# Stage A of a chunked Fourier transform in plain float32, in the four 64x64 quarters of the tensor array, in place of a three-product split-float32r form

## The chip, the cores and the metric

One core of a Trainium2 chip runs one program: a tensor engine (PE, with its weight loads listed as PEld), a vector engine (DVE), a scalar engine (ACT), GpSimd (POOL) and a sync engine (SP) that mostly issues transfers. The metric is the device time of one execution in microseconds, lower is better; three runs were made of the kernel before. Every instruction, transfer and semaphore wait of one execution is in the trace, and a one-page profile sums it up. An operation in float32 is written F32 below; F32R is float32r, a float32 format that the tensor engine takes in one pass with fewer mantissa bits, so the kernel splits an F32 number into a high and a low F32R part where it needs full precision.

## The reference

Three layers follow one another. The change touches only the first, and there only its forward transform.

```python
x: (8, 3072, 256)                              # batch, sequence, channels
X = np.fft.rfft(x, axis=1)
y = np.fft.irfft(X * (filt_r + 1j * filt_i), n=3072, axis=1)
# then a token-mixing layer on y
k = relu(xk @ w_k);  v = (k * k) @ w_v;  z = sigmoid(xr @ w_r) * v      # 256 -> 1024 -> 256
# then on all 24576 rows of z
out = max(z @ w1, z @ w2, z @ w3) @ w_out                               # 256 -> 768 -> 256
```

## The kernel before

The transform of length 3072 is cut as 48 x 64, as two stages of matmuls with a stored intermediate. The 64 is itself a pair (j, m) of 2 x 32: sequence index = 64 n + 32 j + m. **Stage A** transforms over n (48 points, real input, 48 real outputs: real and imaginary parts of 24 frequencies g) for each j and m. **Stage B** then works per g on 128 rows, multiplies by the filter, and **stage C** is the inverse of stage B. Stage A writes its output to the DRAM tensor `s1`, stage B reads it from there, stage C writes `s2`, and the later layers read `s2`.

Batch 0 has a transform of its own at the head of the program (`fft_first`, plain F32, nothing else to overlap with). The seven other batches use `fft(b)`: it returns a list of small pieces, and `drive` puts these between the units of the batch before it (the two later layers), each piece having a weight in about microseconds, so that the pieces are spread over that batch in proportion to their weights. The tile framework's scheduler then orders the instructions of each engine. So stage A of batches 1 to 7 runs in between matmuls of the later layers, and the tensor engine always has other work queued.

In `fft(b)` stage A before has 16 steps (`NA = NM // 2`), each for two values of m. Step s loads a tile `xa` of 96 rows (n and j) x 2 x 256 columns (`a_load`, on SP's queue), ACT casts it to the high part `xah`, POOL subtracts to get the low part `xal` (`split`, L178 and L179). One step later `a_mm` runs three F32R matmuls (`mm3`: high weights x high data, high weights x low data, low weights x high data) of 96 rows by 96 outputs by 512 columns into one PSUM bank `pa`, ACT copies the bank to `ao` (L350) and issues the store to `s1` (L351). The 96x96 weight matrix `wa` holds the same 48x48 transform twice, once on the rows of each j, with zeros elsewhere. All matmuls go through the helper `mm` at L153, so the profile names them by their tiles: `pa<-xah,wa_s` and `pa<-xal,wa_s` are stage A, `pa<-x,wa_f` is the plain F32 stage A of batch 0, `pb`, `pe` and `pa<-x,ws` belong to the last layer, `pk`, `pv`, `pr`, `po` to the two later layers, `pb<-xbh,wbc` to stage B.

PSUM has one pool, `ps`, of 8 banks for everything; a bank comes free when ACT or DVE has read it.

Of the kernel before, what the change touches and what calls it, by code (L numbers as in the profile page):

```python
# [9 lines left out]
F32 = mybir.dt.float32  # L10
F32R = mybir.dt.float32r
# [6 lines left out]
N1 = 48  # L18
N2 = 64
NP = 2 * N1  # L20
NG = N1 // 2
NM = N2 // 2
NQ = 4 * NG
NK = 2 * N2


def fft_constants():


    n1 = np.arange(N1)  # L30
    n2 = np.arange(N2)
    wa = np.zeros((NP, 2, 2, NG))
    wi = np.zeros((2, 2, NG, NP))
    for j in range(2):
        for g in range(NG):
            ph = 2 * np.pi * ((n1 * g) % N1) / N1
            if g == 0:
                wa[j::2, 0, j, 0] = 1.0
                wa[j::2, 1, j, 0] = (-1.0) ** n1
                wi[0, j, 0, j::2] = 1.0 / N  # L40
                wi[1, j, 0, j::2] = (-1.0) ** n1 / N
            else:
                wa[j::2, 0, j, g] = np.cos(ph)
                wa[j::2, 1, j, g] = -np.sin(ph)
                wi[0, j, g, j::2] = 2 * np.cos(ph) / N
                wi[1, j, g, j::2] = -2 * np.sin(ph) / N
    wb = np.zeros((2, N2, NG, 2, N2))
    wc = np.zeros((2, N2, NG, 2, N2))
    freq = np.zeros((2, N2, NG), np.int64)
    for g in range(NG):  # L50
        for s in range(N2):
            if g:
                f = g + N1 * s
                th = 2 * np.pi * ((n2 * f) % N) / N
                c, sn = np.cos(th), np.sin(th)
                sg = 1.0 if s < NM else -1.0
                wb[0, :, g, 0, s] = c
                wb[1, :, g, 0, s] = sn
                wb[0, :, g, 1, s] = -sg * sn
                wb[1, :, g, 1, s] = sg * c  # L60
                wc[0, s, g, 0, :] = c
                wc[1, s, g, 0, :] = -sg * sn
                wc[0, s, g, 1, :] = sn
                wc[1, s, g, 1, :] = sg * c
                freq[:, s, g] = f if s < NM else N - f
            else:
                src = 0 if s < NM else 1
                f = N1 * s if s < NM else NG + N1 * (s - NM)
                th = 2 * np.pi * ((n2 * f) % N) / N
                c, sn = np.cos(th), np.sin(th)  # L70
                freq[:, s, g] = f
                if s == 0:
                    wb[0, :, 0, 0, 0] = 1.0
                    wb[0, :, 0, 1, 0] = (-1.0) ** n2
                    wc[0, 0, 0, 0, :] = 1.0
                    wc[1, 0, 0, 0, :] = (-1.0) ** n2
                    freq[1, 0, 0] = N // 2
                else:
                    wb[src, :, 0, 0, s] = c
                    wb[src, :, 0, 1, s] = -sn  # L80
                    wc[0, s, 0, src, :] = 2 * c
                    wc[1, s, 0, src, :] = -2 * sn

    wb = wb.reshape(4, NM, NG, NK).transpose(1, 0, 2, 3)
    wc = wc.reshape(NK, NG, 4, NM).transpose(0, 1, 3, 2)
    return (
        wa.reshape(NP, NQ),
        wi.reshape(NQ, NP),
        wb.reshape(NK, NG, NK),
        wc.reshape(NK, NG, NK),  # L90
        freq.reshape(NK, NG),
    )
# [33 lines left out]
def tile_spectral_moe(ctx: ExitStack, tc, x, filt, ones, wa, wa1, wi, wbc, wb1, wc1, filt1, filt0, mu, w_k, w_v, w_r, w1, w2, w3, w_out, out):  # L126
    nc = tc.nc
    B = x.shape[0]
    P = 128
    C = 256  # L130
# [12 lines left out]
    cpool = ctx.enter_context(tc.tile_pool(name="cpool", bufs=1))  # L143
# [5 lines left out]

    ps = ctx.enter_context(tc.tile_pool(name="ps", bufs=8, space=bass.MemoryType.PSUM))  # L150

    def mm(o, wgt, rhs, start, stop, more=False):
        nc.tensor.matmul(o, lhsT=wgt, rhs=rhs, start=start, stop=stop, skip_group_check=more)  # L153

    def mm3(o, parts, rhs_parts, onto=False, more=False):

# [6 lines left out]
            mm(o, wl, xh, False, k == n - 1, more)  # L163


    wa_s = cpool.tile([NP, 2, NQ], F32R, name="wa_s")
    nc.gpsimd.dma_start(wa_s, wa)
    wi_s = cpool.tile([NQ, 2, NP], F32, name="wi_s")
    mu_s = cpool.tile([P, 2, 2], F32, name="mu_s")
    nmu_s = cpool.tile([P, 2, 2], F32, name="nmu_s")  # L170
# [6 lines left out]
    def split(hi, lo, src, lo_eng=None):  # L177
        nc.scalar.copy(hi, src)  # L178
        (lo_eng or nc.gpsimd).tensor_tensor(lo, src, hi.bitcast(F32), ALU.subtract)  # L179
# [148 lines left out]
    def fft(b):  # L328

        s1 = dp.tile([NM, 4, NG, C], F32, tag="s1", name=f"s1_{b}")  # L330
        s2 = dp.tile([NM, 4, NG, C], F32, tag="s2", name=f"s2_{b}")
        s2_of[b] = s2
        xv = x[b].rearrange("(p m) c -> p m c", m=NM)
        st = {}
        pieces = []

        def a_load(s):
            t = fp.tile([NP, 2, C], F32, tag="fin", name="xa")
            nc.sync.dma_start(t, xv[:, 2 * s : 2 * s + 2, :])
            hi = fp.tile([NP, 2, C], F32R, tag="fhi", name="xah")  # L340
            lo = fp.tile([NP, 2, C], F32R, tag="flo", name="xal")
            split(hi, lo, t, nc.gpsimd)
            st["a", s] = hi, lo

        def a_mm(s):
            hi, lo = st.pop(("a", s))
            p = ps.tile([NQ, 2, C], F32, tag="pm", name="pa")
            mm3(p, [(wa_s[:, 0], wa_s[:, 1])], [(hi, lo)])
            o = fp.tile([NQ, 2, C], F32, tag="fo", name="ao")
            nc.scalar.copy(o, p)  # L350
            nc.scalar.dma_start(s1[2 * s : 2 * s + 2].rearrange("m r g c -> (r g) m c"), o)  # L351

        NA = NM // 2
        NBS = NG // 2
        for s in range(NA + 1):
            def pa(s=s):
                if s < NA:
                    a_load(s)
                if s >= 1:
                    a_mm(s - 1)  # L360
            pieces.append((0.65, pa))

        def b_load(s):
            w = fp.tile([NK, 4, 2, NK], F32R, tag="wbc", name="wbc")
            if b == 1:

                nc.gpsimd.dma_start(w, wbc[:, s])
                wbc_d[s] = dp.tile([NK, 4, 2, NK], F32, tag=f"wbcd{s}", name=f"wbcd{s}", bufs=1)
                nc.scalar.dma_start(wbc_d[s], w.bitcast(F32))
            else:  # L370
                nc.sync.dma_start(w.bitcast(F32), wbc_d[s])
            f = fp.tile([NK, 2, 2, C], F32, tag="filt", name="filt")
            nc.sync.dma_start(f, filt[:, s])
            t = fp.tile([NK, 2, C], F32, tag="fin", name="xb")
            nc.sync.dma_start(t, s1.rearrange("m r g c -> (m r) g c")[:, 2 * s : 2 * s + 2, :])
            hi = fp.tile([NK, 2, C], F32R, tag="fhi", name="xbh")
            lo = fp.tile([NK, 2, C], F32R, tag="flo", name="xbl")
            split(hi, lo, t)
            st["b", s] = w, f, hi, lo

        def b_mm(s):
            w, f, hi, lo = st.pop(("b", s))
            p = ps.tile([NK, 2, C], F32, tag="pm", name="pb")
            for g in range(2):
                mm3(p[:, g], [(w[:, 0, g], w[:, 1, g])], [(hi[:, g], lo[:, g])], g > 0, True)

            fr, fi = f[:, 0], f[:, 1]
            H = NK // 2
            nc.vector.scalar_tensor_tensor(fi[:H], p[H:], -1.0, fi[:H], ALU.mult, ALU.mult)
            nc.vector.tensor_tensor(fi[H:], p[:H], fi[H:], ALU.mult)  # L390
            nc.vector.tensor_tensor(fr, p, fr, ALU.mult)
            (nc.gpsimd).tensor_tensor(fr, fr, fi, ALU.add)
            yh = fp.tile([NK, 2, C], F32R, tag="fhi", name="yh")
            yl = fp.tile([NK, 2, C], F32R, tag="flo", name="yl")
            split(yh, yl, fr)
            st["c", s] = w, yh, yl

        def c_mm(s):
            w, yh, yl = st.pop(("c", s))
            p = ps.tile([NK, 2, C], F32, tag="pm", name="pc")  # L400
            for g in range(2):
                mm3(p[:, g], [(w[:, 2, g], w[:, 3, g])], [(yh[:, g], yl[:, g])], g > 0, True)
            o = fp.tile([NK, 2, C], F32, tag="fo", name="co")
            nc.scalar.copy(o, p)
            nc.scalar.dma_start(s2.rearrange("m r g c -> (m r) g c")[:, 2 * s : 2 * s + 2, :], o)

        for s in range(NBS + 2):
            def pb(s=s):
                if s < NBS:
                    b_load(s)  # L410
                if 1 <= s <= NBS:
                    b_mm(s - 1)
            def pc(s=s):
                if s >= 2:
                    c_mm(s - 2)
            pieces.append((0.65, pb))
            if s == 0:

                pieces.append((6.0, lambda: None))
            pieces.append((0.65, pc))  # L420
        return pieces
# [520 lines left out]
def layout(x, filt_r, filt_i, mu_k, mu_r, w_k, w_v, w_r, w1, w2, w3, w_out):  # L942
    wa, wi, wb, wc, freq = fft_constants()
    C = x.shape[2]
    wah = np.stack(two_parts(wa), axis=1)
    wis = np.zeros((NQ, 2, NP), np.float32)
    wis[:, 0] = wi
    wis[:, 1, 1:] = wi[:, :-1]
# [19 lines left out]
```

## Time and profile before

| | |
|---|---|
| median of three runs | 3239.52 us (3239.22 to 3243.35) |
| span of the profiled execution | 3228.3 us |
| PE busy | 3117.6 us (97%), 19256 matmul records |
| ACT, POOL, DVE busy | 1918.9, 1865.8, 1774.2 us (59%, 58%, 55%) |
| stage A of batches 1 to 7 | 336 F32R matmuls, 112 casts, 112 subtractions, 112 copies |

The page gives the span of the profiled execution from its first to its last instruction. The time of a run holds what lies around the span as well: 3239.52 - 3228.3 = 11.2 us between the median and the span. Busy time of the tensor engine counts the modelled end of each matmul, which lies behind the start of the next one, so how often matmuls start is read from the timeline and not from the mean duration.

### The profile page before, as it was taken

The page shows a single profiled execution, that of the slowest core. Times are in us where ns is not written, and L with a number is a line of the kernel's source. Part 1 is how long each engine was busy: PE and PEld are TensorE (multiplying, and loading weights), DVE is VectorE, ACT ScalarE, POOL GpSimd, SP SyncE. Part 2 cuts the span into 40 slices and gives each one's busy share as a digit, 9 for nine tenths or more (in the row PEclk, how much of TensorE's full clock was granted, in tenths as well). Part 3 has the DMA queues.
Part 4 walks back from the last instruction along what each step waited for, and adds up shares of the span by engine and source line. Part 5 has one row for each costly group of instructions (what it writes and reads, how often), then busy time and mean ns, then how long its engine had stood idle before and what let it go on. Part 6 is the DMA issues. An engine that isn't in the chain of part 4 may idle for free.

```text
span 3228.3 us, 55882 instructions
## 1 busy us (share of the span) xinstructions
PE 3117.6 (97%) x19256; PEld 3039.7 (94%) x19256; DVE 1774.2 (55%) x2882; ACT 1918.9 (59%) x4024; POOL 1865.8 (58%) x1619
## 2 busy tenths in 40 slices
PE   6799899999999999999999999999999999999998
PEld 4799889999999999999999999999999999999998
DVE  4865554556554565456545465445654456555554
ACT  5556556656566566656566556665656666555554
POOL 3545665557555675546756566565655567544443
PEclk8899999999999999999999999999999999999999
DMA  8767786657765676657766577655876657655553
GB/s 283 239 231 220 227 299 202 194 174 259 238 196 187 208 244 201 214 170 234 252 196 186 179 252 246 198 187 166 271 237 189 190 191 242 197 162 163 169 163 123
DMA packets 397783, 676.38 MB, mean 210 GB/s; under 512 B 41920, under 2 KB 153664, under 8 KB 396864
## 3 DMA queue, kind: packets, MB, share of 16 engines
q1 hardware_dynamic: 328336, 585.61, 57.1%
q10 hardware_dynamic: 66752, 78.75, 7.1%
q0 software_dynamic: 2416, 8.46, 0.9%
q8 instruction: 156, 2.56, 0.3%
q14 instruction: 123, 1.01, 0.1%
HBM read 580.51 MB, written 92.14 MB: 208 GB/s over the span
## 4 chain that ended last, share of the span: by engine, by line
PE 79%; DMA 8%; DVE 7%; issue 2%; ACT 2%; POOL 2%; SPq 0%; ACTq 0%; POOLq 0%; DVEq 0%
PE pb L153 18%; PE pk L153 13%; PE pv L153 13%; PE po L153 12%; PE pe L153 8%; PE pa L153 6%; PE pr L153 4%; PE py L153 3%; DMA wbc<-wbcd 3%; DMA ws<-wud 2%; PE pc L153 2%; DVE x L179 1%; DVE sc L665 1%; DMA wbc<-in_wbc 1%; POOL klo L179 1%
## 5 line engine op out<-in xcount | busy, mean ns | idle before, releaser
L153 PE MATMUL pb<-x,ws 128*128 128x384 f32 x3456 | 759.9, 339 | 15.6 <-DMA ws<-wud 12.4
L179 POOL TENSOR_TENSOR hh<-m,hh 128x384 fp32r<-128x384 f32 x384 | 398.7, 1046 | 557.4 <-ACT hh L178 446.1
L179 POOL TENSOR_TENSOR klo<-kr,khi 128x384 fp32r<-128x384 f32 x492 | 518.2, 1060 | 261.0 <-ACT khi L178 246.6
L153 PEld LDWEIGHTS pb<-x,ws 128*128 128x128 f32 x3456 | 600.7, 189 | 31.8 <-ACT u L701 7.1
L633 DVE SCALAR_TENSOR_TENSOR kr<-pk,kr 128x384 f32<-128x384 f32 x512 | 282.1, 554 | 496.3 <-ACT kr L632 495.0
L153 PE MATMUL po<-wo_hi,hh 128*128 128x256 f32 x2304 | 484.9, 283 | 5.9 <-ACT hh L178 3.3
L153 PE MATMUL pv<-khi,ws 128*128 128x384 f32 x2048 | 475.8, 338 | 7.3 <-ACT khi L178 7.2
L153 PEld LDWEIGHTS po<-wo_hi,hh 128*128 128x128 f32 x2304 | 391.3, 190 | 11.1 <-ACT hh L178 6.9
L153 PE MATMUL pe<-x,ws 128*128 128x384 f32 x1728 | 388.6, 337 | 0.0
L178 ACT CAST khi<-kr 128x384 fp32r<-128x384 f32 x512 | 260.6, 512 | 193.3 <-DVE kr L633 164.9
L153 PEld LDWEIGHTS pv<-khi,ws 128*128 128x128 f32 x2048 | 359.8, 188 | 12.7 <-ACT khi L178 11.9
L153 PE MATMUL pk<-xh,wk_hi 128*128 128x384 f32 x1024 | 341.4, 337 | 3.9 <-ACT xh L178 3.9
L153 PE MATMUL pk<-xl,wk_hi 128*128 128x384 f32 x1024 | 344.1, 336 | 0.2 <-DVE xl L179 0.2
L153 PE MATMUL pk<-xh,wk_lo 128*128 128x384 f32 x1024 | 344.0, 336 | 0.0
L632 ACT ACTIVATE kr<-pk 128x384 f32<-128x384 f32 x512 | 249.2, 489 | 117.1 <-PE pk L153 55.8
L153 PE MATMUL po<-wo_lo,hh 128*128 128x256 f32 x1152 | 317.5, 282 | 0.0
L748 DVE TENSOR_TENSOR m<-sc,m 128x384 f32<-128x384 f32 x384 | 311.5, 814 | 10.0
L153 PEld LDWEIGHTS pe<-x,ws 128*128 128x128 f32 x1728 | 298.8, 189 | 0.9 <-DVE sc L747 0.2
L153 PE MATMUL pv<-klo,ws 128*128 128x384 f32 x1024 | 293.0, 338 | 3.9 <-POOL klo L179 3.0
L179 POOL TENSOR_TENSOR xl<-xm,xh 128x768 fp32r<-128x768 f32 x126 | 233.6, 1869 | 101.3 <-ACT xh L178 101.3
L178 ACT CAST hh<-m 128x384 fp32r<-128x384 f32 x384 | 193.8, 515 | 147.9 <-DVE m L748 80.4
L701 ACT COPY v<-pb 128x384 f32<-128x384 f32 x288 | 138.5, 481 | 162.0 <-PE pb L153 156.5
(129 smaller groups left out, 6060.0 us busy)
## 6 DMA issues: line engine op xcount, KB each, us to landing
ws<-wud SPq DMA_DIRECT2D x864, 256.0 KB, 3.4
ws<-wvd SPq DMA_DIRECT2D x512, 256.0 KB, 3.2
filt<-in_filt SPq DMA_DIRECT2D x84, 512.0 KB, 5.1
ws<-wud SPq DMA_DIRECT2D x288, 128.0 KB, 3.5
wbc<-wbcd SPq DMA_DIRECT2D x72, 512.0 KB, 5.1
cin<-s SPq DMA_DIRECT2D x64, 384.0 KB, 4.2
out_dram<-osb ACTq DMA_DIRECT2D x192, 128.0 KB, 3.0
xb<-s SPq DMA_DIRECT2D x85, 256.0 KB, 3.5
```

The costliest lines, as they stand in the source:

```text
L153: nc.tensor.matmul(o, lhsT=wgt, rhs=rhs, start=start, stop=stop, skip_group_check=more)
L178: nc.scalar.copy(hi, src)
L179: (lo_eng or nc.gpsimd).tensor_tensor(lo, src, hi.bitcast(F32), ALU.subtract)
L632: nc.scalar.activation(r, p, AF.Relu)
L633: nc.vector.scalar_tensor_tensor(r, p, 0.0, r, ALU.max, ALU.mult)
L665: eng.tensor_tensor(t, a, b, ALU.subtract)
L701: nc.scalar.copy(st[to], st[of])
L748: nc.vector.tensor_tensor(m, c, m, ALU.max)
```

## The change

Stage A of batches 1 to 7 takes x as it is. A step now covers four values of m: the tile `xa` is 128 rows by 4 x 256, of which rows 0 to 47 hold j = 0 and rows 64 to 111 hold j = 1, loaded by two transfers. The weights are one 48x48 matrix, padded to 48x64, at rows 0 to 47 and again at rows 64 to 111. Four F32 matmuls, each of 48 rows by 64 outputs by 512 columns, are placed by `tile_position` in the four 64x64 quarters of the array: rows by j, columns by c (which half of the four m). The two j write to two PSUM banks. Two copies of 128 x 512 and four stores follow. The casts and the subtractions are gone, as are the buffers of `xah` and `xal`; `xa` takes turns in the buffer named `filt`. The weights of `s1`'s rows in stage B (`wb`) and the matrix of batch 0 are permuted to the new order of rows, which moves no instruction.

```diff
     def mm(o, wgt, rhs, start, stop, more=False, at=None):
-        nc.tensor.matmul(o, lhsT=wgt, rhs=rhs, start=start, stop=stop, skip_group_check=more)
+        nc.tensor.matmul(o, lhsT=wgt, rhs=rhs, start=start, stop=stop, skip_group_check=more, tile_position=at)
...
-    wa_s = cpool.tile([NP, 2, NQ], F32R, name="wa_s")
-    nc.gpsimd.dma_start(wa_s, wa)
+    wa_s = cpool.tile([P, P // 2], F32, name="wa_s")
+    nc.scalar.dma_start(wa_s, wa)
...
-        xv = x[b].rearrange("(p m) c -> p m c", m=NM)
+        xv = x[b].rearrange("(n j m) c -> j n m c", j=2, m=NM)
+        R = P // 2
...
         def a_load(s):
-            t = fp.tile([NP, 2, C], F32, tag="fin", name="xa")
-            nc.sync.dma_start(t, xv[:, 2 * s : 2 * s + 2, :])
-            hi = fp.tile([NP, 2, C], F32R, tag="fhi", name="xah")
-            lo = fp.tile([NP, 2, C], F32R, tag="flo", name="xal")
-            split(hi, lo, t, nc.gpsimd)
-            st["a", s] = hi, lo
+            t = fp.tile([P, 4, C], F32, tag="filt", name="xa")
+            for j in range(2):
+                nc.sync.dma_start(t[j * R : j * R + N1], xv[j][:, 4 * s : 4 * s + 4, :])
+            st["x", s] = t
 
         def a_mm(s):
-            hi, lo = st.pop(("a", s))
-            p = ps.tile([NQ, 2, C], F32, tag="pm", name="pa")
-            mm3(p, [(wa_s[:, 0], wa_s[:, 1])], [(hi, lo)])
-            o = fp.tile([NQ, 2, C], F32, tag="fo", name="ao")
-            nc.scalar.copy(o, p)
-            nc.scalar.dma_start(s1[2 * s : 2 * s + 2].rearrange("m r g c -> (r g) m c"), o)
-
-        NA = NM // 2
+            t = st.pop(("x", s))
+            p = [ps.tile([P, 2, C], F32, tag="pm", name="pa") for _ in range(2)]
+            for c in range(2):
+                for j in range(2):
+                    rows = slice(j * R, j * R + N1)
+                    mm(p[j][c * R : c * R + R], wa_s[rows], t[rows, 2 * c : 2 * c + 2], True, True, True, (j * R, c * R))
+            for j in range(2):
+                o = fp.tile([P, 2, C], F32, tag="fo", name="ao")
+                nc.scalar.copy(o, p[j])
+                for c in range(2):
+                    m = 4 * s + 2 * c
+                    nc.scalar.dma_start(s1[m : m + 2, 2 * j : 2 * j + 2].rearrange("m r g c -> (r g) m c"), o[c * R : c * R + N1])
+
+        NA = NM // 4
...
-            pieces.append((0.65, pa))
+            pieces.append((1.0, pa))
```

The scheduler decides where the matmuls of a step come to stand on the tensor engine. The rows below are the start of stage A of batch 1 on that engine. Before, the three matmuls of a step stand together; `pb_`, `pa_` and `pe_` with numbers are PSUM banks of the last layer:

```order
L153 MATMUL pe_2003<-x_1672,ws 128x384 x3
L153 MATMUL pa<-xah,wa_s 96x512
L153 MATMUL pa<-xal,wa_s 96x512
L153 MATMUL pa<-xah,wa_s 96x512
L153 MATMUL pb_2054<-x_1654,ws 128x384 x3
L153 MATMUL pb_1995<-x_1661,ws 128x384 x3
```

Of the change, the same place on the tensor engine, with the first two steps of stage A:

```order
L153 MATMUL pe_2046<-x_1672,ws 128x384 x3
L153 MATMUL pa<-xa,wa_s 64x512 x2
L153 MATMUL pb_2038<-x_1661,ws 128x384 x3
L153 MATMUL pa_2039<-x_1664,ws 128x384 x3
L153 MATMUL pa<-xa,wa_s 64x512 x2
L153 MATMUL pb_1950<-x_1675,ws 128x384 x3
...
L153 MATMUL pe_2113<-x_1672,ws 128x384 x3
L153 MATMUL pa<-xa,wa_s 64x512 x4
L153 MATMUL pe_2046<-x_1678,ws 128x384 x3
```

The four matmuls of the first step are torn into two pairs with six other matmuls between them (each pair holds the two column quarters of one j, that is of one PSUM bank); the four of the second step stand together. Over the whole program 34 of the 56 steps stand as one group of four, 16 as two pairs and 6 as a three and a one: 78 groups, each with whole-array matmuls ahead of it and behind it. Of the 34 groups of four, 21 take both columns of j = 0 first and 13 alternate between the two j.

On ACT, in the same stretch, before:

```order
L350 COPY ao<-pa 96x512
L178 CAST xah<-xa 96x512
L351 DMA s_1_665<-ao 96x2x256
L738 COPY m<-pb_1950 128x384
```

and of the change:

```order
L353 COPY ao<-pa 128x512
L356 DMA s_1_665<-ao 48x2x256 x2
L353 COPY ao<-pa 128x512
L178 CAST hh<-m 128x384
```

The cast is gone from ACT, and there are two store issues for one.

## Rows read from the trace of the kernel before

**Rows 1.** The page: span, busy shares, granted clock by slices of the span

```profile
span 3228.3 us, 55882 instructions
...
PE 3117.6 (97%) x19256; PEld 3039.7 (94%) x19256; DVE 1774.2 (55%) x2882; ACT 1918.9 (59%) x4024; POOL 1865.8 (58%) x1619
...
PEclk8899999999999999999999999999999999999999
```

**Rows 2.** Windows of one batch: stage A, the pause, stages B and C, the rest

```profile
core 0: us, PE busy (x) PEld busy (x) DVE busy (x) ACT busy (x) POOL busy (x), PEclk, DMA share, GB/s
894.00:998.00 104.00, 102.98 (x619) 99.26 (x618) 52.62 (x86) 68.04 (x144) 63.00 (x54) 1.00 0.63 192
998.00:1070.00 72.00, 71.38 (x455) 70.77 (x454) 37.63 (x65) 42.39 (x91) 33.58 (x32) 1.00 0.58 184
1070.00:1247.00 177.00, 172.72 (x1096) 170.49 (x1095) 107.32 (x171) 105.53 (x222) 118.76 (x100) 0.99 0.73 240
1247.00:1281.00 34.00, 34.00 (x217) 34.00 (x216) 13.30 (x26) 20.47 (x44) 20.06 (x19) 1.00 0.57 178
```

**Rows 3.** Timeline of PE around one step of stage A: start, duration in us

```profile
226.84 0.40 PE L153 MATMUL pa<-xah,wa_s 96*96 96x512 f32 x1
227.08 0.39 PE L153 MATMUL pa<-xal,wa_s 96*96 96x512 f32 x1
227.31 0.40 PE L153 MATMUL pa<-xah,wa_s 96*96 96x512 f32 x1
227.54 0.69 PE L153 MATMUL pb<-x,ws 128*128 128x384 f32 x3
```

**Rows 4.** Groups of PE instructions: stage A of batches 1 to 7, then of batch 0

```profile
L153 PE MATMUL pa<-xah,wa_s 96*96 96x512 f32 x224 | 88.8, 396 | 0.5 <-DVE kr L633 0.5
L153 PE MATMUL pa<-xal,wa_s 96*96 96x512 f32 x112 | 43.9, 392 | 0.0
L153 PE MATMUL pa<-x,wa_f 96*96 96x512 f32 x32 | 15.6, 652 | 2.4 <-DMA x<-in_x 2.4
```

**Rows 5.** Timeline of weight loads in stage A of batch 0, and one F32 matmul

```profile
19.23 0.16 PEld L153 LDWEIGHTS pa<-x,wa_f 96*96 96x96 f32 x1 [0.27 <-issue]
...
22.23 0.16 PEld L153 LDWEIGHTS pa<-x,wa_f 96*96 96x96 f32 x1 [0.27 <-issue]
...
20.09 0.59 PE L153 MATMUL pa<-x,wa_f 96*96 96x512 f32 x1
```

**Rows 6.** Timeline of weight loads around the step of Rows 3

```profile
226.50 0.19 PEld L153 LDWEIGHTS pe<-x,ws 128*128 128x128 f32 x1
226.67 0.16 PEld L153 LDWEIGHTS pa<-xah,wa_s 96*96 96x96 f32 x1
226.85 0.17 PEld L153 LDWEIGHTS pa<-xal,wa_s 96*96 96x96 f32 x1
```

**Rows 7.** Waits of PE from 220 us on: total us, times, longest

```profile
PE pb L153 <- DMA wbc<-wbcd: 20.9, 14, 2.8
PE pb L153 <- DMA ws<-wud: 12.4, 14, 2.9
PE pb L153 <- DMA wbc<-in_wbc: 8.4, 6, 2.3
PE pv L153 <- ACT khi L178: 3.6, 10, 0.5
```

**Rows 8.** Groups on ACT and POOL, and transfers, of stage A

```profile
L178 ACT CAST xah<-xa 96x512 fp32r<-96x512 f32 x112 | 69.6, 621 | 5.5 <-DMA xa<-in_x 5.5
L350 ACT COPY ao<-pa 96x512 f32<-96x512 f32 x112 | 65.1, 581 | 52.9 <-PE pa L153 51.4 <-PE pb L153 1.5
L179 POOL TENSOR_TENSOR xal<-xa,xah 96x512 fp32r<-96x512 f32 x112 | 150.4, 1343 | 134.1 <-ACT xah L178 128.8 <-PE ps L153 3.5 <-issue 1.8
L351 ACTq DMA_DIRECT2D s<-ao x112: 311/312/383, 228.4 to 2548.0; - x112
xa<-in_x SPq DMA_DIRECT2D x112, 192.0 KB, 3.6
```

More of the change, by code (lines that the diff above doesn't have):

```diff
@@ L82, in fft_constants @@
                     wc[1, s, 0, src, :] = -2 * sn
-    wb = wb.reshape(4, NM, NG, NK).transpose(1, 0, 2, 3)
+    wb = wb.reshape(2, 2, NM, NG, NK).transpose(2, 1, 0, 3, 4)
     wc = wc.reshape(NK, NG, 4, NM).transpose(0, 1, 3, 2)
     return (
-        wa.reshape(NP, NQ),
+        wa.transpose(0, 2, 1, 3).reshape(NP, NQ),
         wi.reshape(NQ, NP),
@@ L150, in tile_spectral_moe, with mm @@
     ps = ctx.enter_context(tc.tile_pool(name="ps", bufs=8, space=bass.MemoryType.PSUM))
-    def mm(o, wgt, rhs, start, stop, more=False):
-        nc.tensor.matmul(o, lhsT=wgt, rhs=rhs, start=start, stop=stop, skip_group_check=more)
+    def mm(o, wgt, rhs, start, stop, more=False, at=None):
+        nc.tensor.matmul(o, lhsT=wgt, rhs=rhs, start=start, stop=stop, skip_group_check=more, tile_position=at)
     def mm3(o, parts, rhs_parts, onto=False, more=False):
@@ L944, in layout @@
     C = x.shape[2]
-    wah = np.stack(two_parts(wa), axis=1)
+    w48 = wa.reshape(N1, 2, 2, 2 * NG)[:, 0, 0]
+    wat = np.zeros((128, 64))
+    wat[:N1, :N1] = wat[64 : 64 + N1, :N1] = w48
+    wah = wat.astype(np.float32)
     wis = np.zeros((NQ, 2, NP), np.float32)
```

## Prediction

> **What bounds the kernel now.** First the page: the tensor engine is busy for 97% of the span and its clock is granted in full after the first two slices, while ACT, POOL and DVE are each below 60% [rows 1]. Next the windows of one batch, by stage. In the stretch that holds stage A the tensor engine is busy 102.98 of 104 us; in the pause and in the rest it is as full; only where stages B and C run is it idle for 4.3 us of 177 [rows 2]. So in the stage that changes, the tensor engine is the limit, and nothing else can give much: 1.0 us of idle time a batch, 7 us over seven. The list of waits says the same for the whole program: its largest entries are transfers of stage B's weights and of the last layer's, and the largest one on ACT is 3.6 us [rows 7]. A step of stage A is therefore worth the time during which it holds the array, and that is read from the starts in the timeline, not from the mean durations: three F32R matmuls start at 226.84, 227.08 and 227.31 and the next one behind them at 227.54 [rows 3]. That is 0.70 us a step, or 0.233 us for 512 columns.
>
> **What is removed.** 16 steps x 7 batches = 112 steps, 336 matmuls (224 and 112 in the groups [rows 4]): 112 x 0.70 = 78.4 us of the array. 69.6 us of casts leave ACT and 150.4 us of subtractions leave POOL [rows 8]. Neither engine is waited for in stage A by more than the 7 us above, so I value both at 3 us, with 0 and 7 as bounds.
>
> **What is added on the array.** Batch 0 already runs stage A in F32, in the whole array. The code issues 16 matmuls there and the trace has 32 records [rows 4]: an F32 matmul is two passes, each with its own weight load. From the load at 19.23 to that at 22.23 there are eight loads, seven intervals: 3.00 / 7 = 0.4286 us a pass, 0.857 us a matmul of 512 columns [rows 5]. The new stage A has 56 steps of four such matmuls, 224 matmuls and 448 passes. A pass of 48 rows and 64 outputs I cost like the one of 96 by 96, because the number of columns that stream through is the same. All depends on how many passes run side by side, which no row of this trace shows: every matmul in it takes the whole array. The bounds are the four matmuls in the time of one, and one after another.
>
> The two passes of a matmul follow one another in its quarter, and in the timelines matmuls start in the order in which they are written. If that holds between quarters too, the first pass of the second matmul cannot start before the second pass of the first one, and that one waits until its quarter is free. The passes then form a staircase: two passes side by side at a time, and a group of n matmuls takes n + 1 pass times, not 2. For the groups of the new order this is 34 x 5 + 32 x 3 + 6 x 4 + 6 x 2 = 302 pass times, 302 x 0.4286 = 129.4 us: 51.0 us more than the 78.4 us removed. All quarters side by side: 78 groups x 0.857 = 66.9 us, 11.5 us less. One after another: 448 x 0.4286 = 192.0 us, 113.6 us more. I take the staircase, because it needs only what the rows show of order and of passes, and some overlap of quarters.
>
> **What is added around each group.** Before each of the 78 groups and behind it the array changes from whole to quarters and back. Today a load runs under the matmul before it (226.67, 0.17 us ahead of the start of its matmul at 226.84) and a matmul starts 0.16 us before the recorded end of the one ahead of it (0.40 long, next start 0.235 later; in F32 0.59 against 0.43) [rows 3, 5, 6]. If a switch costs nothing, this stays so: 0. If the array must run empty and then load, each group loses 0.16 + 0.16 on entry and 0.16 + 0.19 on exit: 0.67 us, 52 us in all. I take the middle, 0.34 us a group or 26 us, since no row is nearer to one end. [...]
>
> **The rest.** The two copies of a step are as many and as wide as before (112 of 0.58 us [rows 8]; the partitions grow from 96 to 128, the columns don't). ACT issues 224 stores for 112, 112 x 0.312 = 35 us of issue time against 69.6 us of casts: ACT still gains. SP issues 112 loads of 192 KB as before, 3.6 us to land [rows 8], and a step is asked for one piece ahead, now about twice as far apart (104 / 16 = 6.5 us before), so the load stays hidden; were it not, each step would wait for what is left of 3.6 us. `xa` now shares the two buffers of the filter tiles: stage B's first filter load waits for the last matmuls of stage A, but a pause of 72 us lies between [rows 2]. The pieces of stage A weigh 9.0 for 11.05, so stages B and C spread over some 6% more of the batch. Their waits for weights (20.9 + 8.4 us [rows 7]) may move by some us either way; I take 0, bounds -10 and +10. A step now takes two PSUM banks at once, which the torn groups already show.
>
> **Sum.** -78.4 + 129.4 + 26 - 3 = +74 us. The profiled span of 3228.3 becomes 3302, and with the 11.2 us that lie around it the time is 3314 us, 2.3% slower.
>
> **Rivals.**
> 1. All quarters side by side, which ends on the other side. -11.5 us on the array, -3 us elsewhere, plus the switches: 3225 us where these are free, 3277 us where they cost 0.67 us. For it: nothing in the rows says that the second pass of one quarter must hold up another quarter. Against it: starts are in order wherever the trace shows them. It is faster by over 0.2% (6.5 us, about what a measurement of this kernel can tell) only if a switch costs less than (14.5 - 6.5) / 78 = 0.10 us a group. [...]
> 2. The quarters give nothing: 448 passes one after another, +113.6 us and the switches, 3350 to 3402 us. For it: no matmul in the trace ever overlaps another by more than its 0.16 us. Against it: only that the work would fit side by side.
> 3. Only quarters of different rows overlap, columns of the same rows don't. Then a pair of one j takes 4 pass times, the 21 groups that take one j first take 7, the 13 others 5, a three 4, a one 2: 147 + 65 + 128 + 24 + 12 = 376 pass times, 161.2 us, +82.8 us and the switches: 3319 to 3371 us.
>
> **How the numbers follow.** Staircase 0.45, side by side 0.27, only rows 0.13, one after another 0.15. The staircase alone runs from 3277 (switches free, 10 us won elsewhere) to 3348 us. For 8 in 10 the range must take in most of the side-by-side case and of the serial case: I leave out the first below 3232 us (about 0.08) and the second above 3385 us (about 0.08). Faster by over 0.2% needs the first rival with switches under 0.10 us a group, or under 0.23 us if stage B's waits also give their 10 us: half of its 0.27, 0.14, and 0.04 for gains that no row shows, 0.18. Within 0.2%: 0.08, the next slice of that rival. Slower: the rest, 0.74.
>
> **What the next profile would show.** 448 matmul records `pa<-xa,wa_s`. Staircase: in a group of four, starts of first passes about 0.43 us apart and 2.1 us from the first start to the last pass's end; side by side, all four within 0.1 us and 0.86 us in all; serial, 3.4 us. Switch: the gap between the last pass's start plus 0.43 and the start of the whole-array matmul behind it, against 0. POOL's busy time should fall by about 150 us, ACT's by about 70. PE's matmul records should be 19256 - 336 + 448. My forecast is wrong if the starts in a group are closer than one pass, or if the switch costs more than 0.67 us or lets the clock fall.

## The result, and the profile after

The changed kernel takes 3251.49 us (median of four runs, 3247.67 to 3256.93) against 3239.37 us of before: 12 us more by the medians, and a ratio over the runs of 1.0055 with a 95% interval of 1.0034 to 1.0077, which is 18 us (11 to 25). It is slower, as forecast, but by a sixth to a quarter of the forecast 74 us: 3251 lies inside the range of 3232 to 3385 and far below its point of 3314. The profiled execution took 3250.0 us with a span of 3248.2 us. The result lists a fourth run of before, 3229.6 us, and the span of 3228.3 fits that run alone: 1.3 us lie around it, not 11.2 (1.8 us in the changed kernel's profile), and the profile of before was its fastest run. In four later sessions before had a median near 3234 to 3236 us over runs from 3225.6 to 3247.2. So two profiles may differ by 10 us for no reason in the kernels, and times are compared below by ratios of many runs.

The page of the changed kernel answers to [rows 1]:

```profile
span 3248.2 us, 55888 instructions
...
PE 3126.8 (96%) x19368; PEld 2993.6 (92%) x19368; DVE 1777.3 (55%) x2882; ACT 1866.3 (57%) x3912; POOL 1724.9 (53%) x1506
...
PEclk8899999999999999999999999999999999999999
```

19368 = 19256 - 336 + 448 matmul records: two for each F32 matmul, as in batch 0. POOL lost 141 us and ACT 53 us of busy time, and the clock is granted as before (0.990 on average over the span, 0.988 before). Now the timeline of the tensor engine around one group of four, start and duration in us. The second and third row come from a narrow window (236.63 to 236.9 us) that cuts the group open; the others from one over the whole group, so the rows overlap:

```profile
235.98 0.68 PE L153 MATMUL pe<-x,ws 128*128 128x384 f32 x3
236.32 0.34 PE L153 MATMUL pe<-x,ws 128*128 128x384 f32 x1
236.59 0.66 PE L153 MATMUL pa<-xa,wa_s 48*64 48x512 f32 x4
236.59 1.09 PE L153 MATMUL pa<-xa,wa_s 48*64 48x512 f32 x8
237.61 0.80 PE L153 MATMUL pe<-x,ws 128*128 128x384 f32 x3
```

This is what decides the case. Four passes are under way in a window that begins 0.04 us behind the first start, and all eight are over in 1.09 us. The starts in the trace, in ns from one to the next, are 6, 7, 7, 460, 6, 7, 7: one pass in every quarter, and 0.46 us later the other pass in every quarter. There is no staircase. That the close starts belong to different quarters, and not to the two passes of one matmul, shows in the six groups of a single matmul: there the second pass starts 0.48 us behind the first. A pair, which holds two columns of the same rows, has its starts 6 or 7 ns apart too, so columns overlap as well as rows do. The weight loads show the rest of a group's price:

```profile
236.16 0.19 PEld L153 LDWEIGHTS pe<-x,ws 128*128 128x128 f32 x1
236.59 0.21 PEld L153 LDWEIGHTS pa<-xa,wa_s 48*64 48x64 f32 x8 [0.25 <-issue]
237.61 0.47 PEld L153 LDWEIGHTS pe<-x,ws 128*128 128x128 f32 x3 [0.81 <-issue]
```

Before, a load ran under the matmul ahead of it [rows 6]. Here the first load of the group starts no earlier than its matmul's record, and so does the first one behind the group. By starts, over all 78 groups (medians): 0.268 us from the last whole-array start to the group where 0.173 is regular (95 ns lost), 0.500 us inside a group of four and 0.487 in a pair, 0.519 us from its last start to the next whole-array matmul, and that one is followed 0.105 us late (three matmuls last 0.80 us where they last 0.69 elsewhere). So a group takes 0.095 + 0.500 + 0.519 + 0.105 = 1.22 us, a pair 1.21 us, and 0.36 us of it are not passes. The 78 groups take 94.6 us; by the same measure the 112 steps of before took 79.8 us.

The windows of one batch, to be set against [rows 2] (stage A, the pause, stages B and C, the rest):

```profile
904.00:987.00 83.00, 81.99 (x504) 70.56 (x504) 37.54 (x65) 48.55 (x103) 32.60 (x30) 1.00 0.72 214
987.00:1066.00 79.00, 79.00 (x489) 78.81 (x489) 42.32 (x70) 43.75 (x95) 40.19 (x37) 1.00 0.61 184
1066.00:1254.00 188.00, 181.72 (x1166) 179.17 (x1166) 113.61 (x179) 112.69 (x235) 120.98 (x104) 1.00 0.73 231
1254.00:1292.00 38.00, 38.00 (x239) 38.00 (x238) 18.32 (x31) 23.54 (x52) 21.37 (x20) 1.00 0.52 163
```

Stage A got shorter (83 us for 104), and stages B and C longer (188 for 177) with more idle time in them: 6.3 us where there were 4.3. The lengths hold the other layers' matmuls too and go with the weights of the pieces (9.0 for 11.05 in stage A); the four stretches together are 388 us for 387. What the tensor engine waited for shows in its list of waits from 220 us on, against [rows 7]:

```profile
PE pb L153 <- DMA ws<-wud: 25.3, 17, 2.9
PE pb L153 <- DMA wbc<-wbcd: 15.3, 11, 2.1
PE pv L153 <- ACT khi L178: 6.5, 10, 2.3
PE pb L153 <- DMA wbc<-in_wbc: 5.4, 4, 2.4
```

The wait for the last layer's weights has doubled from 12.4 us, and no instruction of stage A is in it. All waits of the list together are 72.7 us after and 58.5 us before.

### The profile page after: what moved, and what is told of

Its sections match the earlier page's. It is cut to its first block, busy times and chain, and to the rows that moved or that the text cites. A ratio compares the mean times of both kernels' runs of the same rounds, so it can differ in the third digit from the quotient of the medians.

```text
span 3248.2 us, 55888 instructions
## 1 busy us (share of the span) xinstructions
PE 3126.8 (96%) x19368; PEld 2993.6 (92%) x19368; DVE 1777.3 (55%) x2882; ACT 1866.3 (57%) x3912; POOL 1724.9 (53%) x1506
## 4 chain that ended last, share of the span: by engine, by line
PE 81%; DMA 8%; DVE 5%; POOL 2%; issue 2%; ACT 2%; ACTq 0%; SPq 0%; POOLq 0%; DVEq 0%
PE pb L153 18%; PE pk L153 14%; PE pv L153 13%; PE po L153 12%; PE pe L153 8%; PE pa L153 7%; PE pr L153 4%; DMA ws<-wud 3%; PE py L153 3%; DMA wbc<-wbcd 2%; PE pc L153 1%; POOL klo L179 1%; DVE sc L670 1%; DMA wbc<-in_wbc 1%; DMA s<-co 1%
## 5 line engine op out<-in xcount | busy, mean ns | idle before, releaser
L153 PE MATMUL pb<-x,ws 128*128 128x384 f32 x3456 | 763.2, 340 | 35.1 <-DMA ws<-wud 25.3
L153 PEld LDWEIGHTS po<-wo_hi,hh 128*128 128x128 f32 x2304 | 393.2, 189 | 25.7 <-issue 14.6
L753 DVE TENSOR_TENSOR m<-sc,m 128x384 f32<-128x384 f32 x384 | 272.2, 714 | 8.2
L612 DVE SCALAR_TENSOR_TENSOR xm<-yt,nmu_s,xm 128x384 f32<-128x384 f32 x256 | 203.0, 829 | 84.0 <-ACT xm L611 84.0
```

The source lines that it names most:

```text
L612: nc.vector.scalar_tensor_tensor(v[:, h], yt[:, h, :, :MC], nmu_s[:, w, h : h + 1], v[:, h], ALU.mult, ALU.add)
L753: nc.vector.tensor_tensor(m, c, m, ALU.max)
```

## The experiments

"PE waits" is the sum of the waits in the list from 220 us on; "array" is what the groups of stage A take by starts, with the late matmul behind each. "Holes" are counted by starts as well: where a matmul elsewhere starts over 40 ns later than is regular behind the one ahead of it, summed from stage A's first matmul of a batch to stage B's first ("A, pause") and from there to stage C's last ("B, C"). Array, holes and those of the rest of the program (70 to 80 us in every run) explain the differences of the profiled spans within 4 us. Each is one profile, and that of before is its fastest run.

| run | ratio to before (95%) | groups | array us | PE waits us | holes A, pause us | holes B, C us |
|---|---|---|---|---|---|---|
| before | 1 | 118 | 79.8 | 58.5 | 23.8 | 71.6 |
| the change | 1.0055 (1.0034 to 1.0077) | 78 | 94.6 | 72.7 | 18.5 | 86.3 |
| whole_groups | 1.0070 (1.0051 to 1.0089) | 56 | 69.3 | 93.9 | 43.9 | 101.2 |
| long_groups | 1.0245 (1.0225 to 1.0264) | 28 | 59.5 | 134.9 | 123.6 | 77.0 |
| pairs | 1.0189 (1.0171 to 1.0207) | 116 | 139.8 | 72.7 | 18.6 | 87.2 |
| f32_whole_array | 1.0003 (0.9992 to 1.0013) | 112 | 98.4 | 56.8 | 13.1 | 72.4 |
| paced | 1.0036 (1.0023 to 1.0049) | 80 | 96.8 | 56.8 | 27.8 | 61.9 |
| f32_whole_splits | 1.0052 (1.0038 to 1.0066) | 112 | 100.2 | 56.7 | 22.5 | 70.0 |
| whole_paced | 0.9959 (0.9945 to 0.9973) | 56 | 68.6 | 60.1 | 25.7 | 68.6 |
| before_light | 1.0083 (1.0063 to 1.0103) | 115 | 82.5 | 77.3 | 19.4 | 98.8 |
| whole_priority | 1.0082 (1.0064 to 1.0101) | 56 | 68.4 | 89.1 | 46.6 | 94.4 |
| whole_paced_15 | 1.0054 (1.0037 to 1.0071) | 56 | 68.2 | 88.0 | 49.0 | 87.4 |
| f32_whole_casts | 1.0023 (1.0012 to 1.0034) | 112 | 97.2 | 56.3 | 15.3 | 77.6 |
| f32_whole_subs | 1.0000 (0.9990 to 1.0009) | 112 | 97.3 | 57.1 | 14.5 | 75.2 |

**The price of a group.** Theory 1 was that the array accounts for the loss; theory 2 that waits in B and C do.

```diff
             p = [ps.tile([P, 2, C], F32, tag="pm", name="pa") for _ in range(2)]
+            marks = [nc.vector.memset(q[:, 0, :1], 0.0) for q in p]
...
+            after_all(group[0], marks)     # the first matmul waits for both memsets
```

> The changed kernel with the four matmuls of every step kept together: 56 groups of four in place of 78 (a one-column memset of each of a step's two PSUM banks, on DVE, holds the first matmul until both banks are free). Theory 1, a group costs 0.87 us of passes side by side and 0.34 us of switching, whatever its size (1.21 us, read from the changed kernel's trace): 22 groups fewer are 26.7 us less than the changed kernel, 3225 us, 0.4% faster than before; each group in the trace takes 1.2 us as now. Theory 2, what the change lost lies in waits of stages B and C that the new spacing and transfers bring, and these stay: the time stays within 8 us of the changed kernel (3244 to 3258).

All 56 groups stood whole and took 69.3 us, as foreseen. But the time was 3263 us, no better than the changed kernel (1.0070 against 1.0055, and the intervals overlap): the waits rose by 21 us, those for `ws` to 35.1 us. Theory 1 is right about the array and wrong about the time. Theory 2's place is half of it: by starts the 25 us won on the array came back as 25 us more of holes in stage A and the pause, and B and C hold 15 us more as well.

The second kernel puts eight matmuls, of two loaded tiles and four banks, behind one another. They are at high priority, the second tile takes turns in the buffers of stage B's weights, and stage A's pieces weigh 10.0 together.

> The changed kernel with steps of eight values of m: 28 groups of eight matmuls, two in each quarter, one behind the other without leaving the quarters. Theory 1: the second four cost only their passes, so a group takes 2 x 0.87 + 0.34 = 2.08 us and 28 of them 58 us: 36 us less than the changed kernel's 94.6 us, 3215 us, 0.7% faster than before. Rival within it, the 0.34 us belong to each four matmuls and not to the switch (their second passes or their loads): 2.4 us a group, 68 us, 3225 us like the groups of four. Theory 2: no better than 3244 us.

The switch is paid once for eight matmuls. The weight loads of one such group fall into rounds, the last two of them 0.43 us apart, one pass time as in the whole array; the long stretch without a load, 0.81 us, comes once, behind the group:

```profile
242.19 0.23 PEld L153 LDWEIGHTS pa<-xa,wa_s 48*64 48x64 f32 x8 [0.25 <-DVE pa L352]
242.68 0.17 PEld L153 LDWEIGHTS pa<-xa,wa_s 48*64 48x64 f32 x4 [0.26 <-ACT u L720]
243.11 0.17 PEld L153 LDWEIGHTS pa<-xa,wa_s 48*64 48x64 f32 x4 [0.26 <-issue]
244.09 0.64 PEld L153 LDWEIGHTS pb<-x,ws 128*128 128x128 f32 x4 [0.81 <-issue]
```

28 groups took 59.5 us for 58 foreseen, so the 0.36 us belong to the switch. The time, 3319 us, was lost in stage A and the pause, with 124 us of holes for 18.5. The list of waits of this run is led by an ACT copy that frees a bank, and ACT's own list says what held up its copies `ao`: the stores of `ao` still under way (third row; 3.1 us, twice, in the changed kernel). Four copies follow one another in a step, and `ao` has two buffers. So the output buffers stand beside the four PSUM banks taken at once as a cause, and no run gave `ao` more of them. The granted clock fell as well: on average 0.978 over the span of this profile, 0.990 over that of the changed kernel.

```profile
PE pb L153 <- ACT v L720: 25.6, 7, 5.0
...
PE pb L153 <- ACT ao L366: 18.0, 7, 3.2
...
ACT ao L366 <- DMA s<-ao: 91.8, 37, 6.2
```

The third kernel gives each j a piece of its own, so that steps fall into pairs.

> The changed kernel with the two j of a step in pieces of their own, so that nearly all matmuls stand in pairs: 116 groups in place of 78, the same 224 matmuls. Theory 1: 38 groups more at 1.21 us are 46 us more than the changed kernel, 3297 us, 1.8% slower than before. Staircase of the prediction, if it held: 116 groups with 340 pass times in place of 302, 16 us more, and 38 switches. Theory 2: within 8 us of the changed kernel.

3298.8 us, 47 us above the changed kernel by the medians and 43 by the ratios, with 45.2 us more on the array (139.8 us) and the same waits (72.7 us) and holes. Theory 1's number to a few us; the staircase's 16 us plus switches would be 30. Where nothing else moves, a group costs 1.2 us of time whether it holds two or four matmuls.

**What the splits had cost.** The kernel before, with one F32 matmul in the whole array for the three, its weights in F32 and the split gone (only the line of the matmul is shown):

```diff
-            mm3(p, [(wa_s[:, 0], wa_s[:, 1])], [(hi, lo)])
+            mm(p, wa_s, t, True, True)
```

> The kernel before with stage A in plain F32 in the whole array: one F32 matmul of 96 rows for three F32R matmuls, no casts, no subtractions, the same steps, loads and stores; no quarters and no switches. Theory 1, the array alone counts: 112 steps of 0.857 us for 112 of 0.70 us, 17.7 us more than before, 3257 us, and the relief of ACT and POOL (69.6 and 150.4 us) gives at most 3 us of it back. Rival, the splits' work on ACT and POOL delayed the array elsewhere: less than 8 us more than before.

The array took 18.6 us more and the kernel only 1 us (-3 to +4). Theory 1 falls here: what goes with the splits is worth some 17 us, not 3. From here on theory 3 stands for the two things that theory 1 leaves out: what dropping the splits gives back off the array, and waits that a wider spacing of stages B and C brings. The splits were put back with unused results, without any other edit:

> The F32 stage A in the whole array, with the casts on ACT and the subtractions on POOL still made and their results unused. Without them that kernel took 1 us more than before, though its array time for stage A is 18.6 us longer in the trace. Theory 3: dropping the splits gave 17 us back off the array, so with them the time is 3252 to 3257 us. Rival: the splits cost nothing and an F32 matmul costs less in this place than its passes show: 3235 to 3240 us.

3249.6 us; the ratio rose from 1.0003 to 1.0052, 16 us of 3234. The upper case, if 2 us under its band in absolute time (before ran 2 us faster in that session). The list of waits doesn't show it (56.7 and 56.8 us). Counted by starts, holes of over 40 ns between whole-array matmuls in stage A's stretches sum to 11.0 us with the splits and 2.3 us without; before has 12.2, of which the list of waits names about half: it passes over short idle times, and a matmul's modelled end (0.33 us for starts 0.17 us apart) covers a hole of up to 0.16 us. In a stage that looked 99% full there were thus some 9 us to be had, which the page's busy time hid in part. With 1.8 us on the array that is 10 of the 16 us; where the rest lies is open. The two halves of the splits apart:

> The F32 stage A in the whole array with only the casts on ACT still made, unused (no subtractions). Without the splits this kernel was 0.03% slower than before, with both parts of them 0.52%, so they cost 16 us together. If ACT is where they hurt (its copies free the PSUM banks that the array waits for), the time is 0.4 to 0.6% above before (3246 to 3254 us); if POOL is, 0 to 0.1%.

> The same with only the subtractions on POOL still made, unused (the loaded tile from itself, no casts). If POOL is where the splits hurt (it makes the low parts that the later matmuls wait for), 0.4 to 0.6% above before (3246 to 3254 us); if ACT is, 0 to 0.1%. If each gives about half, the splits cost as a chain, and no single engine is to blame.

The casts alone cost 0.23% (0.12 to 0.34), 7 us; the subtractions alone nothing (-0.10 to +0.09). The casts lie in neither of their bands, the subtractions in the one that speaks for ACT: ACT is about half of it, POOL by itself none, and the other half needs both. Why both together cost more than their sum was not settled; by starts, stage A's holes are 5.6 and 5.1 us with one of them, and 10.9 with both.

**Where B and C lie.** The changed kernel with one number changed, so that stage A's pieces weigh 11.05 together as before:

```diff
-            pieces.append((1.0, pa))
+            pieces.append((17 * 0.65 / 9, pa))
```

> The changed kernel with the weight of a stage A piece raised from 1.0 to 17 x 0.65 / 9 = 1.228, so that the pieces of stage A together weigh what they weighed before and stages B and C lie as they lay before. Theory 3: of the changed kernel's loss some 15 us are waits in stages B and C (88 us there in its trace against 73 before), and they come from the wider spacing of B's and C's pieces; they go, while the array's part stays (80 groups in place of 78, 97 us): 3236 to 3242 us. Rival: these waits come with any new order of the instructions or with the new loads and stores, and the time stays at 3247 to 3257 us.

3244.0 us against 3234.0 of before in that session: between the two bands. The wait for `ws<-wud` went from 25.3 to 0.9 us and all waits from 72.7 to 56.8, as theory 3 said, but the ratio fell only from 1.0055 to 1.0036, and the two intervals overlap. By starts B and C lost 24 us of holes, but the pause behind stage A gained 19 (4 to 24 us), most of it waits that the list puts down to ACT and POOL; two more groups took 2.2 us. So the spacing moved part of the waiting to another place:

```profile
PE pv L153 <- POOL klo L179: 9.0, 7, 2.3
PE pv L153 <- ACT khi L178: 8.4, 11, 1.1
...
PE pb L153 <- DMA ws<-wud: 0.9, 2, 0.4
```

The converse on the kernel before, again one number:

```diff
-            pieces.append((0.65, pa))
+            pieces.append((9 / 17, pa))
```

> The kernel before with one number changed: the weight of a stage A piece is 9 / 17 = 0.529 in place of 0.65, so that its pieces weigh 9.0 together like those of the changed kernel, and stages B and C are spread as widely as there. Theory 3, the spacing alone brings the waits: stages B and C lose 88 to 100 us in the trace in place of 73, and the kernel is 8 to 16 us slower than before. Rival, the waits came with the quarters, their loads or their banks: within 5 us of before.

3261.0 us, 27 us more (20 to 33), above the expected 8 to 16. Nothing of the transform changed, the array's part by 2.7 us only. By starts B and C hold 99 us of holes for 72, which is the 27 us, and the list of waits looks like the changed kernel's:

```profile
PE pb L153 <- DMA ws<-wud: 21.2, 14, 3.1
PE pb L153 <- DMA wbc<-wbcd: 14.6, 12, 1.6
```

So the weight of a piece, a number that seems to be bookkeeping, is worth more here than the whole of the change. Whole groups of quarters with both edits:

> Groups of four kept whole as in the run before with 56 groups (memset, and the four matmuls at high priority) and the weight of 1.228. Theory 3: 25 us less on the array than the changed kernel and no wider spacing of B and C, against what waiting for two banks costs (25 us more in stage A and the pause in the trace of the run with 56 groups, which the priority may shorten): 3225 to 3240 us. Rival: waiting for two banks costs more than the switches it saves, 3250 us or more.

3221.6 us, 0.41% faster than before (0.27 to 0.55), the only version that beats both. Its holes in stage A and the pause, 25.7 us, are no more than those of the torn groups at the same weight (27.8): at this weight, keeping the groups whole costs nothing there. Its `ws` wait is 2.3 us:

```profile
PE pb L153 <- DMA wbc<-wbcd: 19.9, 15, 2.2
...
PE pb L153 <- DMA ws<-wud: 2.3, 3, 1.4
```

This run also had the groups at high priority. With the priority kept and the weight back at 1.0:

> The fast kernel with whole groups at high priority and weight 1.228, with the weight back at 1.0 as in the change. Theory 3: the spacing was what the earlier run with 56 groups lost, so it returns: B's and C's waits 88 to 103 us, 3235 to 3265 us. Rival, the high priority of the groups was what helped: 3218 to 3228 us.

3261.3 us, waits of 89.1 us, 27.8 us of them for `ws`, and the holes are back in stage A and the pause (46.6 us) and in B and C (94.4). The weight alone makes 40 us between these two; the priority is not what helped. And beyond it:

> The same kernel with a weight of 1.5, stages B and C denser than before. If closer spacing of B and C goes on helping, their waits fall below 70 us and the time to 3213 to 3220 us; if 1.228 was near the best, it comes out at 3221 to 3235 us, with B's waits for its weights above 30 us.

3253.6 us, with 39.8 us of waits for stage B's weights (23.2 and 16.6): too dense in the other way. Of the three values tried 1.228 is the best.

## Why the prediction was wrong

**The bound and what was removed** were right in kind: the array's 79.8 us by the finer measure for 78.4.

**The passes are the step that failed.** "If that holds between quarters too ... the passes then form a staircase": it doesn't hold. Every quarter's first pass starts within 20 ns, ahead of any second pass, so a group of four takes two pass times and not five, a pair two and not three. 129.4 us should have been 66.9, the term of the first rival. With it the prediction's own sum is -78.4 + 66.9 + 26 - 3 = +11.5 us, or 3251 us, the measured median; that this is so close is partly luck, since the relief and the spacing were both off and in opposite directions. "Slower" came true without the 51 us that were to bring it. Starts in order, read where every matmul takes the whole array, said nothing about matmuls in different quarters. In the trace the quarters' starts lie 6 to 7 ns apart in the groups of four and about 13 in the groups of eight; from the first start to the last one a group of four takes 0.500 us, 0.07 us more than one pass time. All quarters side by side stood in the prediction with a chance of 0.27, too little.

**The switch** came out as forecast, by luck: 0.34 us a group was the middle of two bounds because no row was nearer to one end, and 0.36 us were measured, 28 us for 26. They are 95 ns ahead of the group, 0.07 us inside it, 0.09 us behind it, and 0.105 us of a load that doesn't run early. Together they are about half of the 0.67 us that the prediction priced for an array run empty and loaded again; whether the array runs empty there, no row shows. The array's balance is then 94.6 - 79.8 = +15 us: the switches eat the 13 us that four quarters save. Each of the 22 torn steps pays a second group of 1.21 us, passes and switch, 26.7 us in all: with whole groups the array's part is 69.3 us, below that of before.

**The relief of ACT and POOL** was valued at 3 us with 7 as a bound, from idle time in the windows; it is 16 us in the whole-array pair of runs. The bound came from busy time, and busy time covers short holes, of up to 0.16 us each. In the quarters it was not measured by itself; by starts the changed kernel has 5 us less of holes in stage A and the pause than before.

**The spacing** was taken as 0 with bounds of -10 and +10. On the kernel before, the lighter weight alone costs 27 us. In the changed kernel it shows as 14 us more waiting in the list and 15 us more of holes in B and C, but returning the weight gave only some 6 us back. The terms of the other kernels therefore don't simply add: 15 - 16 + 27 would be 26 us, and 12 to 18 were measured. By starts, in the two profiles themselves, it is 15 us on the array, 15 in B and C, -5 in stage A and the pause and -4 elsewhere, against 20 us between the spans. How the spacing makes the last layer's weights late was not tried: the loads go through SP's queue like those of stages B and C, and no run here moved them.

**The time around the span** was off too: 11.2 us for 1.3, because the median stood beside the span of the fastest run. That leaves the forecast difference as it was. The upper end of the staircase case, 3348 us, is 3350 by the prediction's own terms (3314 + 26 + 10).

## What to carry to other kernels

In this kernel quarter-array matmuls took less of the array when many stood together (1.21 us for a group of two, 1.22 for four, 2.1 for eight); the time followed only with whole groups and the old total weight. Count the groups, at 0.36 us for the way into the quarters and back in this kernel, before counting columns, and look in the program's order for groups that the scheduler tears (here between the two banks of a step). Look at the buffers for all that a longer group writes: with groups of eight the copies into two output buffers waited 91.8 us for stores. An F32 matmul that frees two engines can be even with a split that is faster on the array (here 1.0003 in time, with 18.6 us more on the array); measure the splits by putting them back unused. And where pieces are dealt out by weights, a change of the number of pieces or of their weight is a second edit: hold the total fixed first, and count holes by starts in every stage, because waiting that leaves one stage can come up in another (here 24 us less in B and C, 19 us more in the pause).

## What the runs showed of the hardware

Two-pass F32 matmuls in the four quarters ran side by side pass by pass, starts 6 to 7 ns apart and 0.46 us from the last first pass to the first second pass in a group of four, though the kernel writes both passes of a matmul as one call. A quarter's weight load of 64 columns is recorded at 0.13 us against 0.16 for 96 and 0.19 for 128. Behind an F32 matmul in the whole array (f32_whole_array, near 1673 us) the next matmul's record starts 26 ns after that of the second pass, and the one behind it about 0.58 us later: the pass's time shows in the row of the wrong matmul, so the price is read over the group.
